# Where GpSimd clears the band's buffer, and three parameter steps with their constants as tensors

## The chip, the cores and the metric

The kernel runs on one core of a Trainium2 chip. The metric is the device time of one execution in microseconds (us), as the median of several runs. The engines are TensorE (PE in the profile), VectorE (DVE), ScalarE (ACT), GpSimd (POOL) and SyncE (SP), which here only issues DMAs.

## The reference

Two independent parts share the output, side by side, for 2048 positions of 448 channels.

```python
# A: attention of 16 heads of 28 channels over 8 earlier positions, 2 apart
q, k, v = split(x @ wqkv)
idx = pos[:, None] - 2 * arange(8)[None, :]
logits = einsum("bhsd,bhswd->bhsw", q, k[idx]) * 28 ** -0.5     # -1e9 where idx < 0
a = einsum("bhsw,bhswd->bhsd", softmax(logits), v[idx]) @ wo
# B: a diagonal complex recurrence (S5)
Lam_bar = exp(dt * Lam);  B_bar = ((Lam_bar - 1) / Lam)[:, None] * Bmat
h[t] = Lam_bar * h[t - 1] + B_bar @ x[t]
b = 2 * (h @ Cmat.T).real + x * Dskip
out = concatenate([a, b], -1)
```

## The kernel before

All steps of the kernel are small functions, and one long string, `ORDER`, gives the order in which they are called. No scheduler moves them: the string fixes the order of the instructions on each engine, and an engine runs its own in that order, with semaphore waits where data or buffers need them. In a step's name the digits are its arguments, `@` gives its PSUM banks, and a final `.` or `=` puts an eviction on ScalarE or on VectorE.

Part A is worked in two halves of 1024 positions (`u`). x is transposed to `xT` (the first half by TensorE, steps `XI`, `XA`, `XH`, with evictions `xi`, `xa`, `xh`; the second half by DMA, line 182). `QA`, `QS` and `QK` (lines 385, 373 and 374, and 258) make q and k, which `qk` evicts to `qf` and `kf`. `P` (line 417) multiplies q and shifted k on VectorE, `E_` (lines 429 and 433) sums the products by head on TensorE. The softmax (`sma`, `smb`, `smc`, lines 457 to 477) works on `attn`, and `AL` and `al` spread its weights into a band, `Ak`, that goes through DRAM into `PT` for the product with v (`AV`, line 572). Two of the four bands lie in one buffer, `Ak0`, that must be zero between the weights: `mz` (line 683) clears it on GpSimd, 128x2560 words of 4 bytes. The first to write weights into it is `al1`.

Part B begins with small per-channel parameters on 128 partitions by G = 7 groups. `pa` to `pc` take exponentials. `pe` (lines 639 to 642) makes angles `u4` of 128x35 numbers, and reduces them to one turn by adding and subtracting a large constant, `MAGIC`. `pf` (lines 646 to 648) takes their sines and cosines on ScalarE. `pd_` (lines 633 to 635) makes `fT`, the turns per step, for the tables of `ty` (line 679, ScalarE), `tk` (lines 692 and 694) and `tf` (line 699, VectorE). `pg` (lines 654 to 664) makes the factors `co`, and `ab` (line 860) copies some of them, with signs, to `acol` and `bcol`, the correction factors, in four short steps on GpSimd. They are first read by `hp`, much later. The columns of `cols` hold constants: column 3, `way`, is -1 on the first half of the partitions and 1 on the second; column 5 is MAGIC, which `tk` uses already. `rb` (line 715) makes rotation matrices `R` from `co` on VectorE.

On GpSimd the order is: constants and masks in the first 7 us, `mz`, `ab`, and then nothing until `OZ` and `OP` open new buffers, which are cleared too (lines 968, 988, 990 and 992: `Z`, the bands 2 and 3, `wo`, `PT`). The matmuls of part B (`BU`, `BR`, line 258 again and 773), the scan (`sa`, `sb`, `sd`) and the output matmuls (`C`, line 916; `W_`, line 585) follow. The ORDER around the places that the change touches:

```
... XI1@4 xi10= xi11= QA00@5 WF4 pe pf pd_ ty1 QA01 tk1= QS30@6 tk0= QA11@7 QA10 ty0 tf0
qk000. XA10@2 xa10= XH1@1 XA11@3 xh1. QS20@4 xa11. QS01@0 tk4. ts00 ... pg qk031. qk001. rb0 ...
```

Of the kernel before, what the change touches and what calls it, by code (L numbers as in the profile page):

```python
# [11 lines left out]
ALU = mybir.AluOpType  # L12
# [8 lines left out]
G = 7  # L21
# [6 lines left out]
MAGIC = 12582912.0  # L28
# [4 lines left out]
WU@0 WF0 XI0@1 PP@2 pcopy WF1 WF2 XI2@3 pa WF3 pb pc xi20. xi00= xi01= XI1@4 xi10= xi11= QA00@5 WF4 pe pf pd_ ty1 QA01  # L33
tk1= QS30@6 tk0= QA11@7 QA10 ty0 tf0 qk000. XA10@2 xa10= XH1@1 XA11@3 xh1. QS20@4 xa11. QS01@0 tk4. ts00 QS11@5 qk010.
wj. qk011. ts10 QS31@1 QK040@23 QS21@7 qk020. QK050@54 pg qk031. qk001. rb0 qk030. qk021. ts20 ty4 QK061@10 QK041 tk5.
QK051 V_111@67 QK060 qk041. P000 P001 LC P010 P011 P020 P021 ty5 qk051. qk040. V_110 E_00@34 E_02 E_01 qh001. qk050.
P030 v111. qh000. V_411@25 tf2 P031 P040 v110. ts02 tk3. V_410 QK100@71 v410. QK110@62 qh011. hc0 qh010. P041 QK111
v411. QK101 QK121@05 qk100. qk101. QK120 qk110. E_03 P050 P051 ts12 P060 qk121. E_05 E_04 qk111. QK131@71 qk120. ts22
ty2 QK161@65 P061 E_06 lt00 lt01 TD0 QK160 qh101. hc1 xt2 BD0 QK130 xt0 qk130. qk131. P100 P101 P110 P111 P120 P121
qh110. qh111. xt1 mz qh100. xt3 ci3. P130 QK150@20 QK151 qk151. QK141@34 V_501@71 QK140 qk141. V_500 sma0 ty3 v501.  # L40
V_400@56 E_10@04 E_11 P131 qk140. qk150. P140 P141 P150 v500. ci2. LD CD2 E_12 V_401 V_001@13 v401. V_101@27 v400.
ci0. V_000 v000. V_100 ci1. V_510@65 v101. V_010@17 CD0 P151 smb0 E_13 P160 CD3 E_15 E_14 v001. v100. V_011 v011.
V_511 v511. P161 E_16 lt10 smc0 lt11 v010. TD1 BU200@32 BU100@75 rb3 tk2. tf1 ab v510. CD1 dk. xd3 xd1 sma1 BU101
BU201 BD1 OZ BU001@04 z20. z10. AL1@1 al1. ad1 AL0@6 al0. tk6. ad0 BR21 z21. BU000 z00. BU010@37 BR01 BR11 xd2 ca3 cs3
z11. BU300@16 z01. smb1 BU301 z30= BU011 BU311@20 BU111@54 BR02 BU110 z02= ts01 BR03 z03. ts11 BR12 z12. ts21 ty6 smc1
BU401@13 BU400 z40. BR31 BR13 UP0 y0= BU310 z31= z13. tf3 BR41 UP1 y1= OP pm3 wo ca6 AX@5 ax. sa0 pm0 BR32 z32.
BU210@17 AL2@6 cs6 BR33 z41. ca1 pm1 pm4 al2. BU411@45 z33. ts03 BU211 BR22 sp0 BU410 BR42 AL3@2 z42. sb0 UP3 y3. z22=
sd0 BR23 z23. al3. ca2 BU600@36 BR43 cs1 UP2 z43= ca4 DN0@1 dn0 BU601 z60. sp1 y2= hp010 BU501@40 pm2 UP4 y4= BU610@21
# [15 lines left out]
def kernel(  # L64
# [17 lines left out]
    V = nc.vector  # L82
# [111 lines left out]
    cols = const.tile([128, 6], F32, tag="cols")  # L194
    hpib, phi, sg, way = (cols[:, i:i + 1] for i in range(4))
# [402 lines left out]
    def small(name, *shape):  # L598
        return const.tile([128, *shape], F32, tag=name, name=name)
    P3 = small("P3", 3, G)  # L600
    lre, lim, ld = (P3[:, i] for i in range(3))
    f8, rk, c1t, c2t, co, fT = (small(*a) for a in (("f8", G), ("rk", 5, G), ("c1t", G), ("c2t", G), ("co", T, 2, G), ("fT", G)))
    dt, are, km, u4, k4, sc2 = (small(*a) for a in (("dt", G), ("are", G), ("km", G), ("u4", 5, G), ("k4", 5, G), ("sc2", 2, 5, G)))
# [26 lines left out]

    @op
    def pd_():
        V.tensor_scalar(km[:], f8[:], MAGIC, None, ALU.add)
        V.scalar_tensor_tensor(fT[:], km[:], MAGIC, f8[:], ALU.subtract, ALU.subtract)
        V.tensor_scalar(fT[:], fT[:], way, None, ALU.mult)

    @op
    def pe():
        V.tensor_tensor(u4[:], f8[:].unsqueeze(1).to_broadcast((128, 5, G)), kph[:, 0], ALU.mult)
        V.tensor_tensor(u4[:], u4[:], kph[:, 1], ALU.add)  # L640
        V.tensor_scalar(k4[:], u4[:], MAGIC, None, ALU.add)  # L641
        V.scalar_tensor_tensor(u4[:], k4[:], MAGIC, u4[:], ALU.subtract, ALU.subtract)

    @op
# [390 lines left out]
```

## Time and profile before

| | |
|---|---|
| median of 3 runs | 125.27 us (125.23 to 125.27) |
| profiled execution | 125.23 us |
| its span, first to last instruction | 123.5 us |
| TensorE busy | 117.3 us (95%) |
| VectorE busy | 112.1 us (91%) |
| ScalarE busy | 103.9 us (84%) |
| GpSimd busy | 22.6 us (18%) |
| granted TensorE clock | 1.0 |

Rows of the profile name an instruction by engine, line of the kernel, operation and tile (written tile, arrow, tiles read), with its shape. A start is in us from the span's start. A line can be that of a helper: line 114 is that of most evictions, line 258 that of most matmuls. Square brackets at the end of a row hold the engine's idle time before it and what released it. The ends of matmuls are modelled, and a matmul's row overlaps the next one's.

### The profile page before, as it was taken

Reading aid. Unit: us, or ns where it says so; the run is one execution under the profiler, and the core shown is the slowest. Engines: PE = TensorE matmul, PEld = TensorE weight load, DVE = VectorE, ACT = ScalarE, POOL = GpSimd, SP = SyncE. Lnnn points to the kernel's source line nnn. Section 1 sums busy time; section 2 is a strip of 40 time slices with the busy share of each in tenths; the row PEclk is TensorE's granted clock in tenths of the full one; section 3 lists DMA queues with packets and bytes.
Section 4 is the critical chain, followed back from the end, with each engine's and each line's share of the span. In section 5 each row is a group of like instructions: output and inputs, shape, how many; then the busy total and the mean of one; then the engine's idle time right before and its main releaser. Section 6 shows DMA issues by size and latency. Waiting matters only on the chain.

```text
span 123.5 us, 2878 instructions
## 1 busy us (share of the span) xinstructions
PE 117.3 (95%) x1061; PEld 59.9 (49%) x1071; DVE 112.1 (91%) x198; ACT 103.9 (84%) x200; POOL 22.6 (18%) x49
## 2 busy tenths in 40 slices
PE   6995999999999999999999999999999999999990
PEld 6963444343334353354345444645665555555560
DVE  4389999999999999999999999999999999998461
ACT  0759999998999999999999999999999999980000
POOL 6890300000000000001999930000000000000000
PEclk9999999999999999999999999999999999999999
DMA  3998999999659999779959998999551603436642
GB/s 104 251 277 209 298 275 203 203 175 303 211 117 213 205 218 175 150 167 312 312 117 150 139 261 300 154 123 145 138 122 23 176 0 124 141 113 199 208 149 74
DMA packets 56661, 22.34 MB, mean 181 GB/s; under 512 B 42343, under 2 KB 56103, under 8 KB 56647
## 3 DMA queue, kind: packets, MB, share of 16 engines
q1 hardware_dynamic: 56440, 22.08, 81.9%
q8 instruction: 8, 0.13, 0.4%
q10 hardware_dynamic: 207, 0.07, 0.2%
q14 instruction: 6, 0.05, 0.1%
HBM read 9.86 MB, written 6.37 MB: 131 GB/s over the span
## 4 chain that ended last, share of the span: by engine, by line
PE 82%; ACT 11%; DVE 3%; issue 2%; ACTq 0%; DVEq 0%
PE ps L258 32%; PE ps L916 16%; PE ps L585 10%; PE ps L429 5%; PE ps L572 4%; ACT Z L114 3%; PE ps L773 3%; PE ps L373 2%; PE ps L276 2%; DVE k L641 1%; PE ps L846 1%; PE ps L941 1%; ACT L706 1%; PE ps L374 1%; PE ps L433 1%
## 5 line engine op out<-in xcount | busy, mean ns | idle before, releaser
L417 DVE TENSOR_TENSOR pr<-qf,kf 128x2048 bf16<-128x2048 bf16 x24 | 27.7, 1222 | 0.1
L258 PE MATMUL ps<-xbuf,BT 128*128 128x512 bf16 (+1 forms) x107 | 23.3, 380 | 0.2
L916 PE MATMUL ps<-Cw,Z 128*128 128x448 bf16 x105 | 20.8, 353 | 0.0
L258 PE MATMUL ps<-xT,wq 128*128 128x512 bf16 (+1 forms) x70 | 15.5, 380 | 0.2 <-issue 0.2
L916 PEld LDWEIGHTS <-Z 128*128 128x128 bf16 x105 | 10.3, 98 | 9.5
L258 PEld LDWEIGHTS <-BT 128*128 128x128 bf16 (+1 forms) x112 | 9.0, 97 | 11.7 <-issue 3.2
L585 PE MATMUL ps<-wo,oT 128*128 128x448 bf16 x64 | 13.4, 353 | 0.0
L258 PE MATMUL ps<-wq,xT 128*128 128x448 bf16 (+1 forms) x64 | 12.0, 354 | 0.0
L114 ACT CAST Z<-ps 128x512 bf16<-128x512 f32 (+1 forms) x23 | 11.4, 538 | 0.3 <-PE ps L258 0.2
L992 POOL MEMSET PT<- 128x4320 f32 x3 | 11.0, 3696 | 0.0
L258 PEld LDWEIGHTS <-wq 128*128 128x128 bf16 (+1 forms) x72 | 6.0, 97 | 8.7 <-issue 2.5
L734 ACT ACTIVATE ctmp<-Cw,c2t 64x448 f32<-64x448 bf16 x14 | 9.3, 666 | 0.2
L585 PEld LDWEIGHTS <-oT 128*128 128x128 bf16 x64 | 6.2, 98 | 5.7
L114 ACT CAST oT<-ps 128x512 bf16<-128x512 f32 x15 | 8.2, 628 | 0.0
L114 ACT CAST v_s<-ps 128x448 bf16<-128x448 f32 x16 | 8.2, 537 | 0.0
L968 POOL MEMSET Z<- 128x14 bf16 x1 | 0.1, 110 | 44.4 <-ACT ctmp L734 44.4
L258 PEld LDWEIGHTS <-xT 128*128 128x128 bf16 (+1 forms) x64 | 5.2, 97 | 6.3 <-issue 1.8
L114 ACT CAST qf<-ps 128x512 bf16<-128x512 f32 x12 | 7.0, 591 | 0.5 <-PE ps L258 0.5
L773 PE MATMUL ps<-Z,R 128*128 128x512 bf16 x20 | 7.1, 381 | 0.1
L114 ACT CAST kf<-ps 128x512 bf16<-128x512 f32 x12 | 7.0, 592 | 0.0
L114 ACT CAST ya<-ps 128x448 bf16<-128x448 f32 (+1 forms) x12 | 6.1, 551 | 0.2 <-PE ps L585 0.2
L926 DVE TENSOR_TENSOR xbuf<-ps,xnB 128x384 bf16<-128x384 f32 x8 | 4.4, 552 | 2.0 <-PE ps L916 2.0
(175 smaller groups left out, 231.2 us busy)
## 6 DMA issues: line engine op xcount, KB each, us to landing
PT<-pd SPq DMA_DIRECT2D x16, 156.0 KB, 4.4
out_dram<-ya SPq DMA_DIRECT2D x16, 112.0 KB, 1.7
out_dram<-xbuf SPq DMA_DIRECT2D x15, 112.0 KB, 1.8
pd<-Ak SPq DMA_DIRECT2D x2, 640.0 KB, 3.6
xbuf<-in_A_x_dram SPq DMA_DIRECT2D x2, 448.0 KB, 4.5
xnB<-in_B_x_dram SPq DMA_DIRECT2D x4, 224.0 KB
xnB<-in_B_x_dram SPq DMA_DIRECT2D x4, 192.0 KB, 3.9
pd<-oT SPq DMA_DIRECT2D x1, 640.0 KB, 5.2
```

Of the source, the lines that this page charges most:

```text
L114: (ACT.copy if e == "A" else V.tensor_copy)(o, i)
L258: PE.matmul(o, l, r, start=(first and i == 0), stop=(not first and i == len(pairs) - 1 and not more[s]))
L276: PE.matmul(p[:, 0:128], wz[:], wz[:], start=True, stop=True)
L417: V.tensor_tensor(t[:], q.unsqueeze(1).to_broadcast((128, 4, 512)), k4, ALU.mult)
L429: PE.matmul(acc[s][32 * i:32 * i + 32], E[:, f, ws, :], t[:, i, :], start=(f == 0 and ws == 0), stop=False)
L572: PE.matmul(p[32 * hh:32 * hh + 32, 128 * bl:128 * bl + n], v_s[:, t, 4 * hg + hh, :], PT[:, t % NS, (4 * hg + hh) // HS, (4 * hg + hh) % ...
L585: PE.matmul(p[:, 0:D], late["oT"][:, b // 4, hg, par, 128 * (b % 4):128 * (b % 4) + 128], late["wo"][:, hg, :], start=(hg == 0), stop=(hg ...
L734: ACT.activation(t[a:a + 64, 0:D], Cw[b:b + 64, g, :], ACTF.Copy, scale=c2t[a:a + 64, g:g + 1])
L773: PE.matmul(pp["z", g, j][:], rot(g, 0), late["Z"][:, g, j - 1, :], start=False, stop=True)
L916: PE.matmul(p[:, 0:D], z, Cw[:, g, :], start=(g == 0), stop=(g == G - 1))
L926: V.tensor_tensor(yo[:, 0:384], p[:, 0:384], xP[:, ct, j // 2, 512:896], ALU.add)
L992: POOL.memset(late["PT"][:, 4 * i:4 * i + 4].rearrange("p t g n -> p (t g n)").bitcast(F32), 0.0)
```

## The change

`mz` is called behind `ab`, and both are called right after the loads of C (`LC`) and among the first products `P`, ahead of where either was in ORDER. Since both run on GpSimd, what this changes there is that `ab` comes first and `mz` second. In `pd_` and `pe`, three steps that took a constant or a column as a scalar operand (TENSOR_SCALAR in the profile) take a column of `cols`, broadcast along the row, as a second tensor (TENSOR_TENSOR). The numbers computed stay the same. No other engine's order changes.

```diff
-... qk041. P000 P001 LC P010 P011 P020 P021 ty5 ...
+... qk041. P000 P001 LC P010 ab mz P011 P020 P021 ty5 ...
-... qh110. qh111. xt1 mz qh100. xt3 ci3. ...
+... qh110. qh111. xt1 qh100. xt3 ci3. ...
-... TD1 BU200@32 BU100@75 rb3 tk2. tf1 ab v510. CD1 dk. ...
+... TD1 BU200@32 BU100@75 rb3 tk2. tf1 v510. CD1 dk. ...
     def pd_():
-        V.tensor_scalar(km[:], f8[:], MAGIC, None, ALU.add)
+        V.tensor_tensor(km[:], f8[:], cols[:, 5:6].to_broadcast((128, G)), ALU.add)
         V.scalar_tensor_tensor(fT[:], km[:], MAGIC, f8[:], ALU.subtract, ALU.subtract)
-        V.tensor_scalar(fT[:], fT[:], way, None, ALU.mult)
+        V.tensor_tensor(fT[:], fT[:], way.to_broadcast((128, G)), ALU.mult)
     def pe():
         V.tensor_tensor(u4[:], f8[:].unsqueeze(1).to_broadcast((128, 5, G)), kph[:, 0], ALU.mult)
         V.tensor_tensor(u4[:], u4[:], kph[:, 1], ALU.add)
-        V.tensor_scalar(k4[:], u4[:], MAGIC, None, ALU.add)
+        V.tensor_tensor(k4[:], u4[:], cols[:, 5:6].unsqueeze(2).to_broadcast((128, 5, G)), ALU.add)
         V.scalar_tensor_tensor(u4[:], k4[:], MAGIC, u4[:], ALU.subtract, ALU.subtract)
```

More of the change, by code (lines that the diff above doesn't have):

```diff
@@ L35 @@
 wj. qk011. ts10 QS31@1 QK040@23 QS21@7 qk020. QK050@54 pg qk031. qk001. rb0 qk030. qk021. ts20 ty4 QK061@10 QK041 tk5.
[L36 to L40, printed above, removed]
+QK051 V_111@67 QK060 qk041. P000 P001 LC P010 ab mz P011 P020 P021 ty5 qk051. qk040. V_110 E_00@34 E_02 E_01 qh001.
+qk050. P030 v111. qh000. V_411@25 tf2 P031 P040 v110. ts02 tk3. V_410 QK100@71 v410. QK110@62 qh011. hc0 qh010. P041
+QK111 v411. QK101 QK121@05 qk100. qk101. QK120 qk110. E_03 P050 P051 ts12 P060 qk121. E_05 E_04 qk111. QK131@71 qk120.
+ts22 ty2 QK161@65 P061 E_06 lt00 lt01 TD0 QK160 qh101. hc1 xt2 BD0 QK130 xt0 qk130. qk131. P100 P101 P110 P111 P120
+P121 qh110. qh111. xt1 qh100. xt3 ci3. P130 QK150@20 QK151 qk151. QK141@34 V_501@71 QK140 qk141. V_500 sma0 ty3 v501.
 V_400@56 E_10@04 E_11 P131 qk140. qk150. P140 P141 P150 v500. ci2. LD CD2 E_12 V_401 V_001@13 v401. V_101@27 v400.
 ci0. V_000 v000. V_100 ci1. V_510@65 v101. V_010@17 CD0 P151 smb0 E_13 P160 CD3 E_15 E_14 v001. v100. V_011 v011.
-V_511 v511. P161 E_16 lt10 smc0 lt11 v010. TD1 BU200@32 BU100@75 rb3 tk2. tf1 ab v510. CD1 dk. xd3 xd1 sma1 BU101
-BU201 BD1 OZ BU001@04 z20. z10. AL1@1 al1. ad1 AL0@6 al0. tk6. ad0 BR21 z21. BU000 z00. BU010@37 BR01 BR11 xd2 ca3 cs3
-z11. BU300@16 z01. smb1 BU301 z30= BU011 BU311@20 BU111@54 BR02 BU110 z02= ts01 BR03 z03. ts11 BR12 z12. ts21 ty6 smc1
+V_511 v511. P161 E_16 lt10 smc0 lt11 v010. TD1 BU200@32 BU100@75 rb3 tk2. tf1 v510. CD1 dk. xd3 xd1 sma1 BU101 BU201
+BD1 OZ BU001@04 z20. z10. AL1@1 al1. ad1 AL0@6 al0. tk6. ad0 BR21 z21. BU000 z00. BU010@37 BR01 BR11 xd2 ca3 cs3 z11.
+BU300@16 z01. smb1 BU301 z30= BU011 BU311@20 BU111@54 BR02 BU110 z02= ts01 BR03 z03. ts11 BR12 z12. ts21 ty6 smc1
 BU401@13 BU400 z40. BR31 BR13 UP0 y0= BU310 z31= z13. tf3 BR41 UP1 y1= OP pm3 wo ca6 AX@5 ax. sa0 pm0 BR32 z32.
```

## Prediction

> **What bounds the kernel now.** I read the busy time by stage first, then the waits, then the chain of waits in order of time, and only then the instructions around the place that these point to. In the first two answers a row gives, for a stretch, the stretch's length and the busy time of each engine, or who waited for whom, with the total, the count and the longest, in us.
>
> ```profile
> span 123.5 us, 2878 instructions
> ...
> core 0: us, PE busy (x) PEld busy (x) DVE busy (x) ACT busy (x) POOL busy (x), PEclk, DMA share, GB/s
> 9.00:12.00 3.00, 1.77 (x22) 1.25 (x20) 2.67 (x9) 2.54 (x7) 0.08 (x1) 1.00 0.83 197
> 12.00:24.00 12.00, 11.78 (x76) 4.99 (x77) 11.74 (x22) 11.89 (x25) 1.04 (x4) 1.00 1.03 250
> 24.00:53.00 29.00, 28.74 (x227) 11.80 (x230) 28.66 (x31) 28.23 (x55) 0.00 (x0) 1.00 0.98 195
> 53.00:65.00 12.00, 11.95 (x87) 5.41 (x85) 11.76 (x19) 11.65 (x21) 6.81 (x4) 1.00 0.85 231
> 65.00:84.00 19.00, 18.70 (x242) 9.55 (x244) 18.62 (x38) 18.74 (x38) 7.21 (x4) 1.00 1.23 187
> 84.00:120.00 36.00, 36.00 (x345) 19.96 (x344) 32.99 (x68) 26.65 (x48) 0.00 (x0) 1.00 0.48 127
> ```
>
> ```profile
> ACT sc L646 <- DVE u L642: 1.6, 1, 1.6
> PE ps L374 <- ACT xT L114: 1.4, 1, 1.4
> ACT qf L114 <- PE ps L258: 0.5, 1, 0.5
> ```
>
> From 12 us to 84 us TensorE, VectorE and ScalarE are all three busy for 97% or more of the time, and from 84 us TensorE alone is full. No engine has slack to give back, and a hole costs its whole length wherever it lies. TensorE has one hole of note behind its warm-up: 1.4 us ahead of line 374, in the stretch 9 to 12 us where it is busy for only 1.77 of 3.00 us. ScalarE has its own, 1.6 us ahead of line 646. The chain of waits ties the two together (start, length, what; the bits of issue time between are left out).
>
> ```profile
> 7.39 1.74 DVE k L641
> ...
> 9.15 0.21 DVE u L642
> ...
> 9.38 0.23 ACT sc L646
> ...
> 10.00 0.90 ACT fr L679 x2
> ...
> 10.93 0.58 ACT qf L114
> ...
> 11.54 0.59 ACT xT L114
> ...
> 12.17 0.38 PE ps L374
> ```
>
> One VectorE instruction of 128x35 numbers (line 641, in `pe`) takes 1.74 us; ScalarE's sines wait for it; the evictions queued behind them on ScalarE, the last of which writes xT (`xh1`), come late; TensorE waits for that xT. Everything turns on why line 641 is slow.
>
> ```profile
> 7.16 0.20 DVE L640 TENSOR_TENSOR u<-u,kph 128x35 f32<-128x35 f32 x1
> 7.39 1.73 DVE L641 TENSOR_SCALAR k<-u 128x35 f32<-128x35 f32 x1
> 9.27 0.16 DVE L633 TENSOR_SCALAR km<-f 128x7 f32<-128x7 f32 x1
> 9.66 0.23 DVE L635 TENSOR_SCALAR fT<-fT,cols 128x7 f32<-128x7 f32 x1
> 12.84 0.17 DVE L658 TENSOR_TENSOR den<-sq 128x7 f32<-128x7 f32 x1
> ```
>
> ```profile
> 6.85 2.23 POOL L683 MEMSET Ak<- 128x2560 f32 x1
> 12.51 0.61 POOL L860 TENSOR_SCALAR acol<-co 64x14 f32<-64x14 f32 x2 [3.43 <-DVE ab L655]
> 13.19 0.57 POOL L860 TENSOR_SCALAR bcol<-co 64x14 f32<-64x14 f32 x2
> 58.19 0.11 POOL L968 MEMSET Z<- 128x14 bf16 x1 [44.43 <-ACT ctmp L734]
> ...
> 54.19 1.09 ACT L114 CAST Ak<-ps 128x512 bf16<-128x512 f32 x2
> ```
>
> GpSimd's memset of the band's buffer (`mz`, line 683) runs from 6.85 to 9.08 us. Line 641 starts inside it and ends at 9.12, 0.04 us behind it. Line 640, a TENSOR_TENSOR of the same size wholly inside the memset, takes 0.20 us; line 633, a TENSOR_SCALAR just after the memset, takes 0.16. So I read it this way: while the memset runs, a TENSOR_SCALAR is held to its end, and a TENSOR_TENSOR is not.
>
> **The change part by part.**
>
> *The three steps become TENSOR_TENSOR.* Line 641 falls from 1.73 us to the 0.20 of line 640, a gain of 1.53 on VectorE and on whoever waits for it. Lines 633 and 635 go from 0.16 and 0.23 us to about the 0.17 of line 658: minus 0.05 us together, beside ScalarE's sines, so I count nothing. The Trainium skill, page "VectorE: DVE Perf Modes", section "The perf-mode tier table", speaks against this part: in fp32 it gives tensor_tensor one element per cycle and tensor_scalar two; by the formula in its errata section, (35+151)/0.96, line 641 would take an estimated 194 ns. The measured 0.20 us of line 640 agrees, and the sum is the same by either.
>
> *The memset moves.* On GpSimd it now stands behind the four `ab` steps (line 860) instead of ahead of them; the order on TensorE, ScalarE and SyncE is unchanged. `ab` waits for the coefficients `co` from VectorE; its four steps take from 12.51 to 13.76 us now. All of this comes 1.53 us earlier, so the memset would run from about 12.23 to 14.46. Behind it on GpSimd stands nothing until the clearing of Z at 58 us; its buffer is first written by the attention product's evictions (line 114) at 54.19 us, some 40 us later. The wait that `mz` newly inherits thus costs nothing. Either part by itself would free line 641: without the memset beside it there is nothing to be held by, and as TENSOR_TENSOR it isn't held.
>
> *What ends the wait next.*
>
> ```profile
> 6.53 1.28 ACT L646 ACT_TABLE_LOAD   x1
> ...
> 9.96 0.81 PE L373 MATMUL ps<-xT,wq 128*128 128x512 bf16 x3
> 12.17 0.38 PE L374 MATMUL ps<-xT,wzz 128*128 128x512 bf16 x1 [1.40 <-ACT xT L114]
> ```
>
> On ScalarE the sines start at 9.38 - 1.53 = 7.85 us; the table load that stands ahead of them ends at 7.81, so it takes nothing off the gain, but the gain can grow no further. The same ScalarE work then puts xT at 12.13 - 1.53 = 10.60 us. TensorE could not start line 374 before about 10.6 to 10.77: three matmuls of line 373 start at 9.96 and 12.17 - 1.40 = 10.77 is where its idle time begins. So TensorE moves up by 1.40 to 1.53 us. VectorE moves with it: its line 699, its eviction of xT and `pg` wait for the same fT and the same sines. I take 1.5.
>
> From there on every stage is the same work with no idle engine, moved up as a block. What does not move is the loads that are already under way. The first that could be late is xT's second half, transposed by DMA (columns: min/median/max ns to issue, first and last start; then us to landing).
>
> ```profile
> L182 SPq DMA_TRANSPOSE xT<-xbuf x4: 1283/1296/1338, 15.5 to 19.6; - x4
> ...
> xbuf<-xnB SPq DMA_TRANSPOSE x4, 4.8
> Cw<-Cn SPq DMA_TRANSPOSE x4, 2.7
> ...
> L727 SPq DMA_TRANSPOSE Cw<-Cn x4: 1227/1274/1722, 47.1 to 52.8; - x4
> ...
> 24.85 2.75 PE L258 MATMUL ps<-xT,wq 128*128 128x512 bf16 x11
> ```
>
> The last of the four is issued at 19.6 us, and its landing isn't shown. By the nearest rows it lands 2.7 to 4.8 us later, at 22.3 to 24.4. TensorE wants it at 24.85 - 1.5 = 23.35 us. So it costs nothing at one end and 1.05 us at the other. I take nothing: it takes as long to issue (1.30 us) as the Cw transposes (1.27) that land in 2.7.
>
> The sum is made against the profiled execution: it took 125.23 us, its span of 123.5 and 1.73 around it, and the median of the three runs is 125.27, 0.04 higher. 125.23 - 1.5 = **123.7 us**.
>
> **The rivals.**
>
> *Slower: the memset holds VectorE in its new place.* It would run from 12.23 to 14.46 us, and VectorE then does this work, 1.53 us earlier than here:
>
> ```profile
> 13.75 1.08 DVE L715 TENSOR_TENSOR R<-Is,co 128x896 bf16<-128x896 bf16 x1
> 14.75 8.25 DVE L417 TENSOR_TENSOR pr<-qf,kf 128x2048 bf16<-128x2048 bf16 x7
> ...
> 59.02 7.34 POOL L992 MEMSET PT<- 128x4320 f32 x2
> ...
> L477 DVE TENSOR_TENSOR attn<-attn,z x2: 1224/1224/1224, 51.9 to 63.6; 128x1024 bf16<-128x1024 bf16 x2
> ```
>
> If a bf16 TENSOR_TENSOR were held as line 641 was, line 715 would start at 14.46 instead of 12.22, and the products behind it with it. VectorE would lose 2.24 and have gained 1.53: 0.7 us later than before, with no idle time up to 84 us to absorb it, and 125.23 + 0.7 = 125.9 us. It decides from a hold of 1.53 us on; with less, the kernel still gains. Against it: line 477 takes 1224 ns at 51.9 us with GpSimd idle and 1224 ns at 63.6 inside the PT memsets (59.02 to 66.36). The Trainium skill, page "SBUF — State Buffer", section "Who interferes with whom", says the same in a rule: a VectorE step with two SBUF inputs contends with a GpSimd step that reads SBUF, not with one that only writes, as a memset does. By that rule, which the rows of line 477 bear out, this rival falls away. For it stands only that lines 715 and 417 have not been seen beside a memset. I give it 9 in 100.
>
> *Smaller: the xT transposes become the wait.* If the last lands at 24.4 us, TensorE waits up to 1.05 us there and 0.45 of the gain is left: 124.8 us. For it: the DMA queue is busy throughout 12 to 24 us (share 1.03). Against: the issue time above. 12 in 100.
>
> *None: line 641 is slow in itself.* The trace has only this one TENSOR_SCALAR of 35 elements; if its length came from its place in the queue and not from its form or the memset, the new form would be as long, and the time 125.2. Against it are the 0.04 us between the two ends, and line 640. 5 in 100.
>
> **How the numbers follow.** The forecast, the whole hole gone, has 74 in 100: 1.40 to 1.55 us, so 123.7 to 123.8, with some 0.2 us for the small shifts that a moved block meets. The range takes in the smaller case too: 123.4 to 124.8 leaves out 14 in 100, the none and the slower case. About 0.2% (0.25 us) is what a measurement can tell from no change. Faster by more than that: 74 + 12 = 0.86. Within it: 0.05. Slower: 0.09.
>
> **What would show it.** Right: line 641 at about 0.2 us; ScalarE's wait ahead of line 646 down from 1.6 us to under 0.1; TensorE's wait at line 374 gone or under 0.2; the memset of Ak at about 12.2 us; lines 715 and 417 at 1.08 and 1.22 us apiece beside it; from there on all rows some 1.5 us earlier, to the last. Wrong: line 715, or the first of line 417, lengthened to the memset's end (slower); a TensorE wait of some tenths ahead of the first 128x512 matmuls of line 258 on xT at about 23 us (smaller); line 641 still long (none). If the front moves up by 1.5 us and the end by less, the time has gone in a load whose landing no view shows, and the stage where rows stop being 1.5 us earlier names it.

## The result, and the profile after

The changed kernel takes 124.50 us (median of 14 executions, 123.66 to 125.36), the kernel before, on the same chip, 125.24 us (median of 14, 125.21 to 125.29). The ratio of the means is 0.9937, with an interval of 0.9913 to 0.9961. So the median gains 0.74 us where 1.5 was forecast, and something new comes with it: the executions of the kernel before lie within 0.08 us, those of the changed one are spread over 1.7.

The profiled execution happens to be the fastest of the 14: 123.66 us, with a span of 121.9. It shows the change at its best, nearly as forecast, and it can't show what the other executions lose. First it, by stage (length of the stretch, then the busy time of each engine, as in the prediction):

```profile
9.00:12.00 3.00, 3.00 (x28) 1.86 (x27) 2.52 (x12) 2.93 (x6) 0.95 (x4) 1.00 0.91 240
12.00:24.00 12.00, 12.00 (x80) 5.09 (x78) 11.80 (x13) 11.92 (x25) 2.26 (x2) 1.00 1.07 234
24.00:53.00 29.00, 29.00 (x256) 12.05 (x255) 28.65 (x32) 28.01 (x55) 0.00 (x0) 1.00 1.06 209
...
65.00:84.00 19.00, 19.00 (x241) 9.53 (x239) 18.65 (x38) 18.75 (x38) 5.54 (x3) 1.00 1.19 184
```

TensorE, busy for 1.77 of 3.00 us in the first of these stretches before, is now full in it, and full in those that follow. The waits of TensorE (who waited for whom: total, count, longest) say the same: the 1.4 us at line 374 are gone. What is left behind the warm-up is 0.4 us for a load of weights.

```profile
PE ps L276 <- DVE wz L120: 1.1, 1, 1.1
PE ps L386 <- DMA wzz<-in_A_wqkv_dram: 0.4, 1, 0.4
```

The front of the same execution, in order of time, engine by engine (start, length):

```profile
6.99 0.20 DVE L641 TENSOR_TENSOR k<-u,cols 128x35 f32<-128x35 f32 x1
7.22 0.20 DVE L642 SCALAR_TENSOR_TENSOR u<-k,u 128x35 f32<-128x35 f32 x1
7.33 0.16 DVE L633 TENSOR_TENSOR km<-f,cols 128x7 f32<-128x7 f32 x1
...
6.51 1.28 ACT L646 ACT_TABLE_LOAD   x1
7.80 0.23 ACT L646 ACTIVATE sc<-u 128x35 f32<-128x35 f32 x1
...
6.61 0.28 PE L386 MATMUL ps<-xT,wzz 128*128 128x256 bf16 x1 [0.38 <-DMA wzz<-in_A_wqkv_dram]
...
10.58 0.38 PE L374 MATMUL ps<-xT,wzz 128*128 128x512 bf16 x1
...
10.85 0.61 POOL L860 TENSOR_SCALAR acol<-co 64x14 f32<-64x14 f32 x2 [3.94 <-DVE ab L655]
11.52 0.57 POOL L860 TENSOR_SCALAR bcol<-co 64x14 f32<-64x14 f32 x2
12.04 2.23 POOL L683 MEMSET Ak<- 128x2560 f32 x1
```

Line 641 takes 0.20 us, the sines of line 646 start without a wait, and line 374 comes at 10.58 us instead of 12.17. The memset has its new place, 12.04 to 14.27 us. Beside it run line 715 and the first products of line 417 (count, then min/median/max ns, first and last start):

```profile
L715 DVE TENSOR_TENSOR R<-Is,co x2: 1082/1084/1086, 12.1 to 51.5; 128x896 bf16<-128x896 bf16 x2
L417 DVE TENSOR_TENSOR pr<-qf,kf x24: 1216/1219/1226, 13.1 to 44.4; 128x2048 bf16<-128x2048 bf16 x24
```

The first line 715, beside the memset, and the second, 39 us later with GpSimd idle, differ by 4 ns at most, and no product of line 417 is lengthened. Later, TensorE's first matmuls on the second half of xT and on part B's x, and the last instruction of the chain:

```profile
23.26 1.46 PE L258 MATMUL ps<-xT,wq 128*128 128x512 bf16 x6
...
48.29 3.08 PE L258 MATMUL ps<-xbuf,BT 128*128 128x512 bf16 x14
...
118.98 0.39 DVE L951 TENSOR_TENSOR xbuf<-ps,xnB 128x224 bf16<-128x224 f32 x1 [0.28 <-PE ps L941]
```

In the kernel before the first of these rows started at 24.85 us. In this execution of the changed kernel the whole block has moved up by 1.59 to 1.60 us; the other two rows in the kernel before:

```profile
49.89 1.47 PE L258 MATMUL ps<-xbuf,BT 128*128 128x512 bf16 x5
...
120.57 0.39 DVE L951 TENSOR_TENSOR xbuf<-ps,xnB 128x224 bf16<-128x224 f32 x1 [0.28 <-PE ps L941]
```

### The profile page after: what moved, and what is told of

Same layout as the page of the kernel before. It is cut to its first block, busy times and chain, and to the rows that moved or that the text cites. A ratio compares the mean times of both kernels' runs of the same rounds, so it can differ in the third digit from the quotient of the medians.

```text
span 121.9 us, 2888 instructions
## 1 busy us (share of the span) xinstructions
PE 117.4 (96%) x1071; PEld 59.3 (49%) x1071; DVE 110.5 (91%) x198; ACT 103.9 (85%) x200; POOL 22.6 (19%) x49
## 4 chain that ended last, share of the span: by engine, by line
PE 92%; DMA 4%; ACTq 1%; DVE 0%; issue 0%
PE ps L258 40%; PE ps L916 16%; PE ps L585 10%; PE ps L429 5%; PE ps L773 4%; PE ps L572 4%; DMA wzz<-in_A_wqkv_dram 4%; PE ps L373 3%; PE ps L846 1%; PE ps L941 1%; PE ps L374 1%; PE ps L433 1%; ACTq L150 1%; PE ps L499 1%; PE ps L385 1%; PE ps L785 1%
## 5 line engine op out<-in xcount | busy, mean ns | idle before, releaser
L417 DVE TENSOR_TENSOR pr<-qf,kf 128x2048 bf16<-128x2048 bf16 x24 | 27.7, 1219 | 0.2 <-ACT qf L114 0.2
L258 PE MATMUL ps<-xbuf,BT 128*128 128x512 bf16 (+1 forms) x112 | 24.1, 380 | 0.0
```

The lines of the kernel that those rows point to most:

```text
L258: PE.matmul(o, l, r, start=(first and i == 0), stop=(not first and i == len(pairs) - 1 and not more[s]))
L417: V.tensor_tensor(t[:], q.unsqueeze(1).to_broadcast((128, 4, 512)), k4, ALU.mult)
```

## The experiments: what held line 641

**The move alone.** The memset and `ab` stand where the change puts them; the three steps keep their scalar operands.

```diff
 (ORDER as in the changed kernel)
-        V.tensor_tensor(k4[:], u4[:], cols[:, 5:6].unsqueeze(2).to_broadcast((128, 5, G)), ALU.add)
+        V.tensor_scalar(k4[:], u4[:], MAGIC, None, ALU.add)
 ... (the same for the two steps of pd_)
```

> Only the memset of the band's buffer moves behind the four short GpSimd steps; the three VectorE steps keep their scalar operands (TENSOR_SCALAR). My theory (a memset on GpSimd holds a TENSOR_SCALAR on VectorE to its end): with no memset beside it line 641 takes 0.2 us, ScalarE's wait ahead of line 646 and TensorE's at line 374 go, and the times are those of the changed kernel: lowest about 123.7 us, median about 124.5. Rival (line 641 is slow in itself and only its new form is quick): line 641 stays at 1.7 us and the time at 125.2.

It took 123.89 us (6 executions, 123.67 to 124.63), a ratio of 0.9882 (0.9868 to 0.9897). Two rows of its trace, from VectorE's and from TensorE's timeline:

```profile
7.52 0.18 DVE L641 TENSOR_SCALAR k<-u 128x35 f32<-128x35 f32 x1
...
7.16 0.50 PE L385 MATMUL ps<-xT,wq 128*128 128x256 bf16 x3 [0.73 <-DMA wq<-in_A_wqkv_dram]
```

The same TENSOR_SCALAR that took 1.73 us beside the memset takes 0.18 without it. It is not slow in itself. The second row is a first hint at where the rest goes: this execution took 124.46 us, and TensorE waited 0.73 us for its first weights. Line 374 came at 11.43 us in it, 0.85 behind the fastest execution of the changed kernel, and its last instruction was 0.81 behind, so all that it lost was lost there.

**The tensors alone.** The three steps as in the changed kernel, the memset and `ab` where they were before.

```diff
 (ORDER as before)
-        V.tensor_scalar(k4[:], u4[:], MAGIC, None, ALU.add)
+        V.tensor_tensor(k4[:], u4[:], cols[:, 5:6].unsqueeze(2).to_broadcast((128, 5, G)), ALU.add)
 ... (the same for the two steps of pd_)
```

> Only the three steps become TENSOR_TENSOR; the memset stays where it was, from 6.85 to 9.08 us. My theory (a memset does not hold a TENSOR_TENSOR): line 641 takes 0.2 us inside the memset, and the times are again those of the changed kernel, lowest about 123.7 us, median about 124.5. Rival (the memset holds whatever VectorE reads or writes there, and the move alone helps): line 641 ends at the memset's end as before, 1.7 us, and the time is 125.2.

It took 124.05 us (8 executions, 123.68 to 125.15), a ratio of 0.9919 (0.9892 to 0.9946). VectorE's and GpSimd's timelines:

```profile
7.52 0.20 DVE L641 TENSOR_TENSOR k<-u,cols 128x35 f32<-128x35 f32 x1
...
6.88 2.23 POOL L683 MEMSET Ak<- 128x2560 f32 x1
```

Line 641 lies wholly inside the memset, 6.88 to 9.11 us, and takes 0.20 us: as a TENSOR_TENSOR it isn't held. So either part alone removes the hole, and the two together do no more than either.

**The memset in two halves, back to back, in the old place.** This asks how long the hold lasts: to the end of the memset that runs, or longer.

```diff
     def mz():
-        POOL.memset(Ak0.rearrange("p k n -> p (k n)").bitcast(F32), 0.0)
+        for i in range(2):
+            POOL.memset(Ak0[:, i].bitcast(F32), 0.0)
```

> The kernel before, with the memset cut into two of 128x1280 words, one behind the other in the same place (some 1.15 us each, 6.85 to about 8.0 and on to about 9.2). My theory (held to the end of the memset that is running): line 641 ends with the first one, at about 8.0 us, and takes about 0.6 us instead of 1.73; the next TENSOR_SCALAR, line 633, which took 0.16 us, now falls into the second memset and is held to its end, about 1 us. The sines start some 1.1 us earlier, but fT comes as late as before, so the tables and the evictions behind them gain little: about 125.2 us. Rival (line 641 is slow in itself, or by its place in the queue): line 641 1.7 us, line 633 0.16 us.

It took 125.30 us in its one execution, as long as the kernel before. GpSimd's and VectorE's timelines:

```profile
6.85 2.27 POOL L684 MEMSET Ak<- 128x1280 f32 x2
...
6.99 2.17 DVE L641 TENSOR_SCALAR k<-u 128x35 f32<-128x35 f32 x1
...
9.30 0.16 DVE L633 TENSOR_SCALAR km<-f 128x7 f32<-128x7 f32 x1
```

This expectation was wrong. Line 641 was to be let go at the end of the first half, near 8.0 us. It was held to 9.16 us, 0.04 behind the end of the second half (9.12): for 2.17 us in all, over two memsets that follow each other without a gap. The Trainium skill, page "SBUF — State Buffer", section "Who interferes with whom", says of a VectorE instruction in a mode that uses two ports and one on GpSimd that whoever issues first keeps the shared ports for the whole instruction. That agrees with the kernel before, where line 641 ended 0.04 us behind its memset; here the hold went past the end of an instruction into the next, and the measurement decides.

**Half of the memset in the old place, half behind `ab`.** With a gap between the halves the hold should be half as long, and so should the hole.

```diff
-... qh110. qh111. xt1 mz qh100. ...        ... rb3 tk2. tf1 ab v510. ...
+... qh110. qh111. xt1 mz0 qh100. ...       ... rb3 tk2. tf1 ab mz1 v510. ...
-    def mz():
-        POOL.memset(Ak0.rearrange("p k n -> p (k n)").bitcast(F32), 0.0)
+    def mz(i):
+        POOL.memset(Ak0[:, i].bitcast(F32), 0.0)
```

> The kernel before, with only half of the memset (128x1280 words, about 1.15 us) in its old place, and the other half behind the four short GpSimd steps. In the kernel with two halves back to back line 641 was held to the end of both, 2.17 us. If the hold lasts until GpSimd's row of memsets ends, line 641 now ends with the one half, at about 8.0 us, and takes 0.6 to 1.0 us by its start; the sines start at about 8.3 us instead of 9.38, and the floor of the times is 125.2 - 1.1 = 124.1, with TensorE's hole at line 374 down to about 0.3 us and with some of the spread of the changed kernel above the floor. If the hold had another cause (the place of line 641 in its queue), it stays at 1.7 to 2.2 us and the time at 125.2.

It took 124.16 us (4 executions, 124.16 to 124.21), a ratio of 0.9915 (0.9898 to 0.9931). GpSimd's, VectorE's and ScalarE's timelines:

```profile
6.85 1.17 POOL L683 MEMSET Ak<- 128x1280 f32 x1
...
7.52 0.53 DVE L641 TENSOR_SCALAR k<-u 128x35 f32<-128x35 f32 x1
...
8.31 0.23 ACT L646 ACTIVATE sc<-u 128x35 f32<-128x35 f32 x1 [0.51 <-DVE u L642]
```

Line 641 ends at 8.05 us, 0.03 behind its half memset; it was expected to take 0.6 us or more and took 0.53. The sines wait 0.51 us instead of 1.6, and the time is 1.1 us lower. The hold follows the length of GpSimd's row of memsets, and the time follows the hold. The narrow spread of these four executions comes back below.

## The experiments: where half of the gain goes

Three explanations stood for the 0.8 us between the fastest execution and the median: (a) the transposes that bring xT's second half are late, as the prediction's smaller case has it; (b) the first weights are late, as in the row of line 385 above, and the hole ahead of line 374 used to hide that; (c) the granted clock. The last needed no run: the clock was 1.0 both in the execution of 123.66 us and in those of 124.65 and 124.87, and 0.996 in the longest, 125.36.

**The changed kernel again, one execution.**

> The changed kernel itself once more, for a second profile. Theory b: the span less the start of the first matmul of line 386 is again 115.3 us (121.94 - 6.61 in the first profile; 122.2 - 6.86 and 122.7 - 7.49 in the two kernels with one part of the change), whatever the span. Theory a or another late stage: the front agrees with the first profile and the difference lies behind 20 us.

This execution took 124.85 us, with a span of 123.1, 1.2 more than the fastest. TensorE's timeline:

```profile
49.56 1.67 PE L258 MATMUL ps<-xbuf,BT 128*128 128x512 bf16 x6 [1.02 <-ACT lt L442]
```

The front is the fastest execution's but for 0.1 to 0.2 us: line 374 comes at 10.76 instead of 10.58, the first matmul on xT's second half at 23.44 instead of 23.26. Then, ahead of the first matmuls of part B (line 258 on xbuf), TensorE waits 1.02 us and is 1.27 behind. The row names ScalarE's `lt`, which was done long before (the two instructions for part A's first half end at 32.56 us; those for the second half start, in the fastest execution, at 48.42 us, behind the first of these matmuls): the wait is for more than one thing, and the other is the DMA that transposes part B's x into `xbuf`. So neither (a) nor (b) alone: there is a third place, some 38 us behind the hole.

These transposes stand on SyncE behind that of `attn`, which waits for part A's logits in `lt`. SyncE's timelines of the kernel before, of the fastest execution and of this one:

```profile
34.00 1.27 SPq L451 DMA_TRANSPOSE attn<-lt  x1
...
39.38 6.45 SPq L746 DMA_TRANSPOSE xbuf<-xnB  x3
```

```profile
32.41 1.27 SPq L451 DMA_TRANSPOSE attn<-lt  x1
...
38.03 6.31 SPq L746 DMA_TRANSPOSE xbuf<-xnB  x3
```

```profile
32.59 1.27 SPq L451 DMA_TRANSPOSE attn<-lt  x1
...
38.09 7.16 SPq L746 DMA_TRANSPOSE xbuf<-xnB  x3
```

So these are not loads that stay where they were: `attn` and the transposes behind it move up with part A, by 1.6 and 1.4 us. What differs is how long they take. From the start of `attn` to the end of the last issue it is 11.8 us in the kernel before, 11.9 in the fastest execution, and 12.7 here.

The front has a part of its own. The four matmuls of line 304, among TensorE's first, take 219 ns each in the fastest execution and 314 here and in the kernel before, with a granted clock of 1.0 in all three. No wait for weights stands ahead of line 374 here, and yet it is 0.18 us late. In the trace of the tensors alone, again with 314 ns and without such a wait, it is 0.33 us late.

**More delay put on both kernels.** Two tiles of x (229 KB) are loaded ahead of the first weights instead of behind them, in the changed kernel and in the kernel before. If the hole hid lateness, the second should not care.

```diff
     SP.dma_start(xnA[:, 2:4], xA_r[:, 2:4])
+    SP.dma_start(xnA[:, 4:6], xA_r[:, 4:6])
     w_load(0, 256, 0, D)
-    SP.dma_start(xnA[:, 4:8], xA_r[:, 4:8])
+    SP.dma_start(xnA[:, 6:8], xA_r[:, 6:8])
```

The changed kernel with it:

> The changed kernel, with half of the next x tiles (229 KB, xnA 4 and 5) issued ahead of the first weights instead of behind them: at the 265 GB/s of the profile's first microseconds the first weights land some 0.9 us later. Theory b (the end now follows the landing of the first weights, which varies from one execution to the next): the times go up by about as much, lowest about 124.5, median about 125.2 to 125.4, and TensorE waits for a load of wq or wzz ahead of 9 us. Rival (the spread of the changed kernel comes from a later stage or from the clock): the times stay at 123.7 to 125.4.

The kernel before with it:

> The same delay of the first weights in the kernel before. Theory b (its hole of 1.4 us at line 374, set by the memset, covers late weights): most executions stay at 125.2, since 0.9 us fits into the hole; only where the weights are late by themselves as well does the time rise, to 126 at most; the hole in the profile is shorter by the delay. Rival (late weights cost the kernel before as much as the changed one): all executions rise by 0.9, to about 126.1.

The changed kernel took 124.90 us (12 executions, 124.02 to 125.81; ratio 0.9974, 0.9944 to 1.0004). The kernel before took 125.33 (12 executions, 125.29 to 126.44, all but one within 0.1, and that one with a granted clock of 0.986; ratio 1.0017, 1.0003 to 1.0031). Lines are numbered one higher in both. TensorE's waits, first of the kernel before with the delay:

```profile
PE ps L386 <- DMA wq<-in_A_wqkv_dram: 1.4, 1, 1.4
...
PE ps L375 <- ACT xT L114: 0.7, 1, 0.7
```

A new wait of 1.4 us for the first weights shrinks the hole from 1.4 to 0.7 us, and line 375 (374 elsewhere) still starts at 12.17 us. The kernel loses 0.1 us. This is the hole at work as a cover. Then the changed kernel with the delay:

```profile
PE ps L259 <- DMA xbuf<-xnB: 1.1, 1, 1.1
...
PE ps L259 <- DMA xT<-xbuf: 0.4, 1, 0.4
```

Here the trace names the third place outright: 1.1 us for the transposes of part B's x, and 0.4 for those of xT. That execution's span, 123.7, is 1.8 above the fastest; its first matmul on xbuf starts at 50.08 us, also 1.8 behind 48.29. Everything is lost ahead of that row and nothing behind it. The weights themselves were not late in this execution (its matmul with `wzz` came at 6.81 us, against 6.61), so of (b) this trace says nothing. The expectation of (b) was missed: the lowest rose by 0.36 us and the median by 0.40, not by 0.9.

**The changed kernel once more, in five rounds.** It ran as the partner of the runs below.

> The changed kernel unchanged, beside the two others on the same chip, so that their medians can be compared: lowest 123.7, median about 124.5, up to 125.4. Where its profile has a longer span than the first one's 121.9, TensorE's waits name the place: a load of wq or wzz ahead of 9 us (b), or the first matmuls on xbuf and BT at 48 to 50 us (d).

It took 124.21 us (6 executions, 123.69 to 125.85; ratio 0.9911, 0.9885 to 0.9937, without the 125.85). TensorE's waits in its profiled execution, the one of 125.85 us:

```profile
PE ps L258 <- ACT lt L442: 1.1, 1, 1.1
PE ps L258 <- DMA xT<-xbuf: 0.4, 1, 0.4
```

These are the two waits of the delayed kernel, and its front is 0.56 us late on top (first matmul with `wzz` at 7.17 us). All 21 executions of the changed kernel together have a median of 124.60 us. Eight lie from 123.66 to 124.07, two at 124.29 and 124.35, eleven from 124.60 up. The distance between the two clusters is about the 1.0 us of the wait at xbuf, and the execution traced in the lower one lacks that wait, the two traced in the upper one have it. That the untraced ones differ for the same reason is argued, not shown.

The stretch from the start of `attn` to the end of the last x transpose separates the traces too. It is 12.5 to 12.7 us in the four with the wait at xbuf (the two of the changed kernel, the delayed one, and the next run), and 11.8 to 11.9 in the eight other traces with the same order of DMAs.

**xT's transposes first.** In the changed kernel SyncE issues the four transposes of xT ahead of the six loads of part B's first x instead of behind them.

```diff
-    x_load(0)
     for t in range(4):
         SP.dma_start(xT[:, 1, :, 128 * t:128 * t + 128], xA1[:, t], transpose=True)
+    x_load(0)
```

> The changed kernel ranges from 123.66 to 125.36 us over its executions, where the kernel before lay within 0.08 us: something that varies from one execution to the next was covered by TensorE's hole of 1.4 us and now shows. Here, in the changed kernel, the four DMA transposes of xT are issued ahead of the six loads of B's x instead of behind them; nothing else changes. Theory a (the transposes land late in some executions, and TensorE waits for them at about 23 us): the median falls to about 123.8 and the spread to a few tenths. Theory b (the first weights land late in some executions, ahead of 9 us): median about 124.5 and spread of 1.5 us as before. Theory c (the granted clock drops for a moment when TensorE has no hole): as b, with clocks under 1.0 beside the longer times.

It took 127.35 us (6 executions, 126.77 to 127.86; ratio 1.0167, 1.0141 to 1.0193): slower than both kernels. SyncE's own timeline, then TensorE's and ScalarE's waits:

```profile
9.71 2.89 SPq L167 DMA_DIRECT2D xbuf<-in_A_x_dram  x3
15.78 5.36 SPq L180 DMA_TRANSPOSE xT<-xbuf  x4
21.19 3.15 SPq L177 DMA_DIRECT2D xnB<-in_B_x_dram  x6
```

```profile
PE ps L258 <- ACT lt L442: 1.2, 1, 1.2
...
ACT Cn L117 <- DMA Cr<-in_B_C_im_dram: 1.8, 1, 1.8
```

The transposes read what line 167 loads, so they could not start before 15.78 us, 0.13 later than in the fastest execution (15.65). The queue stood idle from 12.60 to 15.78 us, and everything behind it came that much later: the loads of part B's x now start at 21.19. The median was expected near 123.8, so put this way explanation (a) gives no cure. But the run shows how little slack the queue of DMAs has.

**The weights first.** In the changed kernel the first `wzz` load is issued on ScalarE's queue ahead of the three loads of part B's parameters.

```diff
+    w_half(0, 0, 256, 0, D, eng=ACT)
     raw = prp.tile(...)
     for i, vec in enumerate((B_Lambda_re, B_Lambda_im, B_log_dt)):
         ACT.dma_start(raw[:, i], ...)
-    w_half(0, 0, 256, 0, D, eng=ACT)
```

> The changed kernel, with the load of the first half of wzz (64 KB, line 145, for which TensorE waits 0.38 us at line 386 in the changed kernel's profile) first on ScalarE's queue, ahead of the three small parameter loads, instead of behind them. Theory b: that load is issued 1.3 us earlier and no longer the last to land; what is left is the landing of wq, so the median falls by some tenths, to 124.0 to 124.3, and the spread stays in part. If the parameter loads, now 0.7 us later, hold the exponentials, the median rises instead. Rival (the spread comes from a later stage): 124.5 and the same spread.

It took 125.96 us (12 executions, 124.88 to 126.74; ratio 1.0037, 1.0002 to 1.0073). TensorE's waits:

```profile
PE ps L611 <- DMA raw<-in_B_Lambda_im_dram: 0.5, 1, 0.5
PE ps L611 <- DMA raw<-in_B_Lambda_re_dram: 0.5, 1, 0.5
PE ps L385 <- DVE xT L114: 0.3, 1, 0.3
```

The wait for weights is gone, but the parameters are late instead, and line 641 starts at 8.45 us. The change of order moves the wait and adds to it. Not all of the time is due to that: in this trace the granted clock is 0.50 from 7.5 to 10.5 us, and the four longest of the twelve executions, 126.26 us and up, are those whose mean clock was 0.982 to 0.986. The eight others, at 1.0, have a median of 125.5 us, still slower than the changed kernel.

**One transpose out of the way of part B's x.** The transpose of `Bn` (`BD0`), which stands between those of x on SyncE, is issued earlier, behind the loads of C. First in the changed kernel, then in the kernel before.

```diff
-... P000 P001 LC P010 ...          ... qh101. hc1 xt2 BD0 QK130 ...
+... P000 P001 LC BD0 P010 ...      ... qh101. hc1 xt2 QK130 ...
```

> The changed kernel with one DMA issued earlier: the first transpose of B's matrix (step BD0, line 722, 2.1 to 2.4 us of the DMA queue) right behind the loads of C, where SyncE stands idle for 2.2 us waiting for the softmax's input, instead of between the transposes of B's x. New theory (d): with the hole gone the DMA queue is the next bound; its loads up to 30 us come at their own time, the transposes of B's x behind them end at 47 to 49 us, and where they are late by as much as in the second profile of the changed kernel (1.02 us ahead of the first matmuls on xbuf and BT, line 258), TensorE waits. With 2 us less ahead of them that wait goes: lowest 123.7 as before, median 123.8 to 124.1, and what is left of the spread comes from the first weights alone. Theory b (the first weights are all of it): median 124.5 and the spread stay.

> The same edit in the kernel before. Theory d: nothing to gain, since there the hole at line 374 is longer than what the DMA queue is late by: 125.2, with its narrow spread. Rival (the earlier transpose is worth time by itself): faster by some tenths.

The changed kernel with it took 124.14 us (11 executions, 123.83 to 125.13; ratio 0.9926, 0.9904 to 0.9949), the kernel before with it 125.26 (10 executions, 125.24 to 126.08, all but one within 0.04; ratio 1.0007, 0.9996 to 1.0019). SyncE's timeline of the former:

```profile
32.62 3.17 SPq L722 DMA_TRANSPOSE BT<-Bn  x1
35.90 1.24 SPq L451 DMA_TRANSPOSE attn<-lt  x1
37.24 8.19 SPq L746 DMA_TRANSPOSE xbuf<-xnB  x4
```

The issue of the moved transpose takes 3.17 us, and the four of x still end at 45.43 us (45.25 in the changed kernel's execution of 124.85 us, 44.34 in its fastest execution). The moved transpose holds back that of `attn`, and all behind it. The work was moved and the end was not. The median is that of the changed kernel within the two intervals, and the expected gain isn't shown. This profiled execution (125.13 us) is 1.55 us behind the fastest at the first matmul on xbuf: its first weights were 0.3 us late; another 0.3 went at xT's second half, whose first matmul came 1.83 us behind the end of the transposes' issue, as in the two traces that name that wait (1.81 and 1.82); VectorE waited 0.6 for the `attn` transpose, now later in the queue, and TensorE then 0.4 for VectorE; the wait at xbuf, without a name here, took 0.4; and some 0.15 is in no view.

No version tried is clearly better than the changed kernel. The move alone has the lowest median, 123.89, but from 6 executions of a time with two clusters: four lie within the changed kernel's lower cluster, two above it, and its interval overlaps that of the changed kernel's second series.

## Why the prediction was right, and where it was not

**Line 641 and the hold: right.** The two single edits show both halves of the reading, that the memset holds a TENSOR_SCALAR and doesn't hold a TENSOR_TENSOR, and that either part by itself frees line 641. The rival "none" is out: 0.18 us for the unchanged form. The small steps at lines 633 and 635 cost 0.16 and 0.17 us, beside other work, as put.

**The memset's new place: right.** It ran from 12.04 to 14.27 us (forecast 12.23 to 14.46), with line 715 at 1084 ns and line 417 at 1219 beside it. The rival "slower" is out, and the rule of the Trainium skill that the prediction set against it (page "SBUF — State Buffer", section "Who interferes with whom") agrees with these rows.

**The front, 1.40 to 1.53 us: right, a little small.** Line 374 moved up by 1.59 us, and ScalarE's table load became the limit of the sines, as the prediction had it: it ends at 7.79 us, and they start at 7.80. What the fastest execution has above the forecast comes from its quicker first matmuls, which the change doesn't touch: line 641 starts at 6.99 us in it, and at 7.39 in the kernel before. In the execution of 124.85 us it starts at 7.52, the sines at 7.98, and line 374 moved up by 1.41.

**"From there on every stage is the same work, moved up as a block": right in the fastest execution only.** It took 123.66 us against the forecast of 123.7; that they agree so closely is in part luck, by the 0.18 us of its front.

**The term that was mis-sized is the loads "already under way": "I take nothing".** It cost 0.8 us in the median and from nothing to 1.7 us in the 14 executions. It failed in three ways. First, the prediction looked at only one load, "the first that could be late", xT's second half. There the reading was near: the last of the four transposes lands about 3.1 us after its issue (issued at 20.9 us in the delayed kernel, matmul released at 24.02), inside the 2.7 to 4.8 it gave. But the start of that issue was taken as fixed at 19.6 us, and it is 19.7, 20.3 and 21.4 in three traces of the changed kernel. The wait was 0.4 us where it appeared, so the smaller case is seen in part. Second, the larger wait, 1.0 to 1.1 us, lies at 49 us, where part B's x is first used. The row for it, `xbuf<-xnB` with 4.8 us to landing, stood in the prediction, used only as a bound for xT. The sum it lacked: the last issue of these transposes ends at 45.83 us before, TensorE wants them at 49.89, so they have 4.06 us to land, and about as much after the move, since both move with part A (44.34 and 48.29 us in the fastest execution, 3.95 apart). In the two traces of the changed kernel with the wait and in that of the delayed one their issue ends 0.6 to 0.8 us later behind `attn`, and they land 4.2 to 4.4 us behind that end. Third, the first weights: 0.73 us in the trace of the move alone, 0.38 in the fastest execution. TensorE's first matmuls, for which the sum had no term, cost 0.18 and 0.33 us in two traces.

That the median still lies in the stated range is partly luck. The range reached up to 124.8 us for xT's transposes, and the larger loss came from other loads.

**What one trace can't show.** The narrow time of the kernel before, 125.23 to 125.27 us, gave no sign that its loads vary. The delay put on that kernel shows that the narrowness was in part a property of the hole: with 1.4 us of idle TensorE behind the first weights, anything ahead of it that is late by less cost nothing there, late weights and slower first matmuls alike (line 304's take 314 ns in the kernel before and 219 in the delayed one, and line 374 comes at 12.17 us in both). For xT's second half, whose transposes did not move (15.54 us before, 15.65 in the fastest execution), the matmuls came 1.6 us later than they do now. Remove the hole, and each execution pays for its own front. Half of the memset left in place fits this. Its hold covered first weights that came 0.47 us late (`wzz` matmul at 7.08 against 6.61), and its four executions lie within 0.05 us. With four, that is a hint, not a proof. For part B's x the cover isn't shown: from the start of `attn` to the first matmul on xbuf it is 15.89 us in the kernel before and 15.88 in the fastest execution. What has shrunk is the distance to the loads ahead of `attn` (the last load of C): its issue ended 3.7 us ahead of `attn` before, and 1.6, 1.5 and 0.4 in the three traces of the changed kernel. That this is what lengthens the transposes is not shown; half of the memset has 0.5 there and no wait.

**Open:** why the DMA queue is late in some executions. The first transposes of xT wait for the loads of line 167 and start anywhere from 15.65 to 17.32 us in three traces of the same kernel. No run here separates the causes of that. Open too is why the x transposes of part B take 0.6 to 0.8 us longer to issue in some executions, and why TensorE's first matmuls are slower in some.

## What to carry to other kernels

A hole in the bottleneck engine hides what is late ahead of it by less than its length, and gives that much more time to those loads behind it that don't move when it goes. Before its whole length is booked as a gain, list each load with the time its landing leaves until it is wanted, at every stage down to the end of the block that moves, note which loads move with the block and which do not, and take a narrow spread of times as a possible sign of cover and not of punctual loads. After such a change one profiled execution is not enough: look at the spread, and trace a typical execution as well as the fastest.

## What the runs showed of the hardware

The hold of a TENSOR_SCALAR of 128x35 numbers by GpSimd's memset ends with the row of memsets, not with the instruction it began in: 2.17 us over two halves back to back (one execution), 0.53 with one half. A TENSOR_TENSOR of the same shape took 0.20 us inside the same memset, and 128x896 and 128x2048 ones in bf16 were unmoved by it. A wait of TensorE for several things can carry the name of one long done: at 49.56 us the row named ScalarE's `lt`, and only the delayed kernel's trace named the transposes. The issue of one DMA transpose of the same x took 1.51 us before and 2.00 and 2.63 in two traces of the changed kernel. And TensorE's first matmuls differ from one execution to the next, 219 or 314 ns for the same 128x128 one, with a granted clock of 1.0 shown for both.
